# TensorE's first work on a tile of ones that VectorE fills, instead of the identity matrix

## The chip, the core and the metric

The kernel runs on one core of one Trainium2 chip. The metric is the device time of one execution in microseconds. Before the change it is 965.68 us, the median of three runs (965.58 to 966.01). Lower is better.

## The reference

Two attention layers read the same input `x` (2048 tokens of 448 numbers, 16 heads of 28), and a gate per token mixes their outputs:

```python
g = sigmoid((x * gate_w).sum(-1, keepdims=True))
return g * A(x) + (1 - g) * B(x)
```

A is linear attention with a learned feature map: each head's query and key go through a 28 x 28 matrix `w_phi`, the features are the softmax of the result beside the softmax of its negative, and the output is phi_q (phi_k^T V) over phi_q (phi_k^T 1). B is full softmax attention, with a 2048 x 2048 matrix of scores for each head and no mask. Both end in an output projection, and all of it is float32.

## The kernel before, in words

The program works through four stages.

The first projects the queries and keys of B. Each float32 operand is split into a high part, rounded to a shorter format (`XH`, `w[:, 0]`), and a low part that holds the rest (`XL`, `w[:, 1]`); a product is the sum of three matmuls, high by high, high by low and low by high. `first_units` (line 614) does this for the first 512 tokens, block by block of the 448 inputs; `proj_qk` (line 568, through the helper `run` at line 109) does it for the rest, copies the result out on ScalarE, subtracts on VectorE for the low part (`keep_qk`, lines 580 and 581), and stores both to memory (line 582). The second stage computes all of A. The third computes the values of B and the first part of the row maxima that the softmax of B needs (`mx_unit`, lines 239 to 273, on the tiles `kp` and `qp`, where line 207 subtracts two loaded tiles from one another). The fourth is a loop of 256 steps that computes scores, exponentials and weighted sums, with the remaining maxima between them.

The order of work on TensorE, VectorE, ScalarE and POOL (GpSimd) is the order in which the program writes it: line 52 names these four engines. The queue of SP (SyncE), which issues all the transfers, isn't among them. Its order is chosen by the planner of the framework when the program is built.

What matters here is the very beginning. Lines 83 and 84 allocate the tile `ident` (128 x 128, float32) and fill it with the identity matrix; `make_identity` issues two POOL instructions for it, a memset and an affine select (the profile shows them as masks.py:197 and masks.py:199). VectorE's first instruction is the memset of `red` at line 163, and POOL goes on with the memset of `part` at line 161. In `first_units`, SP issues eight loads of weights and inputs. Lines 624 and 625 then issue eight matmuls of the identity with itself into the bank of `pqs[3]`. Their result is never read: the first real matmul into that bank, at line 642, starts a new sum. That first matmul needs `w[:, 0]`, which ScalarE copies at line 628 once the weights have landed, and `XH`, which VectorE copies at line 629 once the inputs have landed; for the later blocks ScalarE does both.

The identity is used again by the transposes of lines 515, 528, 1150 and 1160.

Of the kernel before, what the change touches and what calls it, by code (L numbers as in the profile page):

```python
# [8 lines left out]
F32 = mybir.dt.float32  # L9
# [8 lines left out]
P = 128  # L18
# [18 lines left out]
def f32(ap):  # L37
    return ap.bitcast(F32)
# [3 lines left out]
def gated_mix_kernel(ctx, tc, xT, wqkB, wvB, wvA, wkAT, wqAT, phi, woA, woB,  # L42
# [7 lines left out]
    nc = tc.nc  # L50
# [4 lines left out]
    const = ctx.enter_context(tc.tile_pool(name="const", bufs=1))  # L55
# [7 lines left out]
    def ps_s(nm):  # L63
        return ps.tile([P, 512], F32, tag="s", name=nm, bufs=psn[0])

    def ps_pv(nm):
        return ps.tile([P, 512], F32, tag="pv", name=nm, bufs=1)

    def ps_mx(nm):
        return ps.tile([P, 512], F32, tag="mx", name=nm, bufs=psn[1])  # L70
# [11 lines left out]

    ident = const.tile([P, P], F32, name="ident")
    make_identity(nc, ident)
    sel_s = const.tile([P, 4], F32, name="sel_s")
    mask_s = const.tile([112, 64], F32, name="mask_s")
    z_s = const.tile([P, NT], F32, name="z_s")
# [489 lines left out]
    def keep_qk(m, t, pq, ev):  # L577
        tt = slice(t * 512, (t + 1) * 512)
        e = ev.tile([P, 2, 512], F32R, tag="ev", name=f"ev{t}_{m}")
        nc.scalar.copy(e[:, 0, :], pq)  # L580
        nc.vector.tensor_sub(e[:, 1, :], pq, f32(e[:, 0, :]))
        nc.sync.dma_start(qk_d[m * P:(m + 1) * P, :, tt], f32(e))
# [14 lines left out]
    def x_loads(t):  # L597
        loads(("x", t), lambda: load_x(t, 0), lambda: load_x(t, 2))
# [7 lines left out]
    def splits(n):  # L606

        if n % 4 == 1 and n < 12:
            split_x(n // 4 + 1, raws.pop(("x", n // 4 + 1)))
        if n in (13, 15):  # L610
            split_part(wB[1], "wB1", 384, (n - 13) // 2)
        take_lows()

    def first_units():

        raw = [stg.tile([P, 2, 512], F32, tag="stg", name=f"first_raw{b}") for b in range(3)]
        raw.append(f32(ev.tile([P, 2, 512], F32R, tag="ev", name="first_raw3")))
        for b in range(4):
            nc.sync.dma_start(raw[b][:, 0, :], wqkB[:, b, :512])
            nc.sync.dma_start(raw[b][:, 1, :], xT[:, b, :512])  # L620
        x_loads(1)
        pqs = [ps_s(f"pqk0_{m}") for m in range(3)] + [ps_pv("pqk0_3")]
        later.extend(ps_mx(f"pqk_{i}") for i in range(3))
        for _ in range(8):
            nc.tensor.matmul(pqs[3][:, :P], ident, ident, start=True, stop=True)
        for b in range(4):
            w, x = wB[0][:, :, b, :], XH[:, b, :512]
            nc.scalar.copy(w[:, 0, :], raw[b][:, 0, :])
            (nc.scalar.copy if b else nc.vector.tensor_copy)(x, raw[b][:, 1, :])
            nc.vector.tensor_sub(w[:, 1, :], raw[b][:, 0, :], f32(w[:, 0, :]))  # L630
            if b < 3:
                nc.vector.tensor_sub(XL[:, b, :512], raw[b][:, 1, :], f32(x))
                todo = [(0, x), (1, x), (0, XL[:, b, :512])]
            else:
                nc.vector.tensor_sub(x[64:], raw[b][64:, 1, :], f32(x[64:]))
                todo = [(0, x), (1, x)]
            if b < 3:
                order = [(i, m) for i in range(3) for m in range(4)]
            else:
                order = [(i, m) for m in range(4) for i in range(2)]  # L640
            for i, m in order:
                nc.tensor.matmul(pqs[m], w[:, todo[i][0], m * P:(m + 1) * P], todo[i][1],  # L642
                                 start=b == 0 and i == 0, stop=b == 3 and i == 1,
                                 skip_group_check=True)
        hold = raws[("x", 1)][0][:1, 0, :4]
        splits(1)
        nc.gpsimd.tensor_copy(phi_s[:1, :, 0], hold)
        for m in range(4):
            keep_qk(m, 0, pqs[m], ev)

    later = []
    first_units()
    pkv = ps_pv("pkv")
    for n in range(4, NP):
# [644 lines left out]
```

## Time and profile before

| | |
|---|---|
| median of three runs | 965.68 us |
| the profiled execution | 965.82 us |
| its span, first to last instruction | 964.0 us |
| TensorE busy | 959.0 us, 99% of the span |
| ScalarE busy | 741.7 us, 77% |
| VectorE busy | 712.9 us, 74% |
| POOL busy | 230.2 us, 24% |
| granted TensorE clock | 1.000 |

Times are microseconds from the span's start. PE is TensorE's matmuls and PEld its weight loads, DVE is VectorE, ACT is ScalarE, and SPq is SyncE's queue of transfers. Matmuls are pipelined and their ends are modelled, so that two records can overlap; the distance between their starts is the surer measure of pace. A row of the timeline merges neighbours of one kind: its first number is the start of the first, its second the time to the end of the last, and xN says how many there are. In brackets stands how long the engine was idle before, and what ended that.

### The profile page before, as it was taken

The numbers are of one execution on the slowest core, as the hardware profiler recorded it, in microseconds if no ns is written. First come the engines' busy times: TensorE is split into PE (matmuls) and PEld (weight loads), VectorE is DVE, ScalarE is ACT, GpSimd is POOL, SyncE is SP. The second block draws the span as 40 slices with busy tenths as digits, with TensorE's granted clock in tenths as the row PEclk, the third lists the DMA queues.
The fourth block names the chain that finished last, engine by engine and source line by source line (L and its number), as shares of the span: only waits on it lengthen the run. The fifth ranks groups of instructions, "written<-read, shape, count | busy, mean of one in ns | idle before, by whom it ended". The sixth has DMA issues, their size and how long they took to land.

```text
span 964.0 us, 22412 instructions
## 1 busy us (share of the span) xinstructions
PE 959.0 (99%) x8510; PEld 592.7 (61%) x8510; DVE 712.9 (74%) x1338; ACT 741.7 (77%) x1224; POOL 230.2 (24%) x237
## 2 busy tenths in 40 slices
PE   9999999999999999999999999999999999999998
PEld 8877877787877655555554555555555455555555
DVE  5576767789855678888888888888888888885112
ACT  4465656578866788888888898898988988887662
POOL 1235445578734800111101001001101001000010
PEclk9999999999999999999999999999999999999999
DMA  8883110023333334022132121232231222000441
GB/s 299 296 283 121 39 54 33 23 63 98 86 107 101 98 110 138 26 60 55 57 111 57 32 62 50 62 88 61 63 84 46 66 60 76 31 21 32 146 151 58
DMA packets 56620, 84.49 MB, mean 88 GB/s; under 512 B 17696, under 2 KB 24464, under 8 KB 56512
## 3 DMA queue, kind: packets, MB, share of 16 engines
q1 hardware_dynamic: 56512, 83.06, 28.4%
q8 instruction: 67, 1.10, 0.5%
q14 instruction: 41, 0.34, 0.1%
HBM read 54.86 MB, written 27.78 MB: 86 GB/s over the span
## 4 chain that ended last, share of the span: by engine, by line
PE 99%; DVE 0%; POOL 0%; issue 0%; POOLq 0%
PE pv L1061 27%; PE wide L891 18%; PE g L891 10%; PE pqk L109 6%; PE poa L109 4%; PE pk L127 4%; PE pva L127 4%; PE g L289 4%; PE pq L109 4%; PE pmd L261 4%; PE pob L109 3%; PE pvb L127 2%; PE pvb L109 2%; PE pft L528 2%; PE pqk L642 1%; PE pn L541 1%
## 5 line engine op out<-in xcount | busy, mean ns | idle before, releaser
L296 DVE TENSOR_REDUCE part<-g 128x1 f32<-128x512 f32 x704 | 442.8, 685 | 79.7 <-PE g L289 77.6
L900 ACT ACTIVATE pw<-wide 128x1024 f32<-128x1024 f32 x232 | 237.4, 1023 | 58.0 <-PE wide L891 58.0
L903 ACT ACTIVATE p<-g 128x512 f32<-128x512 f32 x510 | 277.7, 605 | 0.0
L1061 PE MATMUL pv<-p,vb 128*32 128x512 f32 x1028 | 270.0, 605 | 0.0
L1061 PE MATMUL pv<-pw,vb 128*32 128x512 f32 x1020 | 268.9, 605 | 0.0
L891 PE MATMUL g<-qst,kst 32*128 32x512 f32 x1668 | 249.9, 411 | 0.0
L891 PEld LDWEIGHTS wide<-qst,kst 32*128 32x128 f32 x1392 | 112.2, 183 | 194.5 <-ACT pw L900 190.3
L289 PE MATMUL g<-kc,qc 28*128 28x512 f32 x704 | 229.7, 489 | 0.0
L891 PE MATMUL wide<-qst,kst 32*128 32x512 f32 x1392 | 224.5, 426 | 0.0
L891 PEld LDWEIGHTS g<-qst,kst 32*128 32x128 f32 x1668 | 159.7, 183 | 21.8 <-ACT pw L903 6.7
L266 DVE CUSTOM_DVE_ANT_0 rl<-pmb,rl 128x512 f32<-128x512 f32 x160 | 103.4, 684 | 49.8 <-ACT rl L265 49.7
L412 POOL TENSOR_TENSOR oUb<-oUb,rsb 128x512 f32<-128x512 f32 x15 | 19.3, 1286 | 480.6 <-DMA rsb<-rdb 358.6
L265 ACT ACTIVATE rl<-pmd 128x512 f32<-128x512 f32 x160 | 87.3, 602 | 32.6 <-PE pmb L261 31.8
L289 PEld LDWEIGHTS g<-kc,qc 28*128 28x128 f32 x704 | 86.6, 182 | 0.1
L1061 PEld LDWEIGHTS pv<-pw,vb 128*32 128x32 f32 x1020 | 37.6, 108 | 36.2 <-issue 32.4
L109 PE MATMUL pqk<-XH,wB 128*128 128x512 f32 x192 | 59.1, 397 | 0.0
L1061 PEld LDWEIGHTS pv<-p,vb 128*32 128x32 f32 x1028 | 37.8, 108 | 29.0 <-issue 28.3
L903 ACT ACTIVATE pw<-g 128x512 f32<-128x512 f32 x46 | 26.0, 642 | 26.9 <-PE g L891 26.5
L580 ACT CAST ev<-pqk 128x512 fp32r<-128x512 f32 x28 | 16.0, 589 | 36.8 <-PE pqk L109 15.5
L109 PE MATMUL poa<-woA_s,oTa 128*128 128x448 f32 x192 | 43.4, 375 | 0.0
L1072 DVE SCALAR_TENSOR_TENSOR acc<-pob,gate,acc 128x448 f32<-128x448 f32 x12 | 8.2, 684 | 47.2 <-PE pob L109 47.2
L109 PEld LDWEIGHTS pqk<-XH,wB 128*128 128x128 f32 x192 | 35.5, 188 | 8.5 <-issue 1.5
(169 smaller groups left out, 1268.7 us busy)
## 6 DMA issues: line engine op xcount, KB each, us to landing
qkd<-ev SPq DMA_DIRECT2D x28, 512.0 KB
qst<-qkd SPq DMA_DIRECT2D x64, 112.0 KB
kst<-qkd SPq DMA_DIRECT2D x64, 112.0 KB
od<-oTb SPq DMA_DIRECT2D x48, 112.0 KB
rsa<-rda SPq DMA_DIRECT2D x32, 128.0 KB
oL<-od SPq DMA_DIRECT2D x8, 512.0 KB
rsb<-rdb SPq DMA_DIRECT2D x15, 256.0 KB
gad<-ga SPq DMA_DIRECT2D x16, 224.0 KB
```

What stands on the lines that cost most here:

```text
L109: nc.tensor.matmul(dst, l, r, start=i == 0, stop=i == len(todo) - 1)
L127: nc.tensor.matmul(dst[:, :n], l, r, start=i == 0, stop=i == len(todo) - 1, skip_group_check=True)
L261: nc.tensor.matmul(pm[j], qc[js, qt * P:(qt + 1) * P], kc[js, :], start=True, stop=True, tile_position=(32 * i, 0))
L265: nc.scalar.activation(rl, pm[i], AF.Relu)
L266: nc.vector.tensor_tensor_reduce(rl, pm[2 + i], rl, 1.0, LOWEST, ALU.add, ALU.max, part[:, col + i:col + i + 1])
L289: nc.tensor.matmul(pm, mxs[("qc", gq)][js, qt * P:(qt + 1) * P], mxs[("kc", gq // NQ, kb)][js, :], start=True, stop=True, tile_position=(3 ...
L296: nc.vector.tensor_reduce(part[:, col:col + 1], pm, AX.X, ALU.max)
L412: (nc.gpsimd if n == 1 else nc.vector).tensor_mul(oU, oU, rs)
L891: nc.tensor.matmul(st[j], kst_of[(gq // NQ, kt // 4)][js, k, (kt % 4) * P:(kt % 4 + 1) * P], qst_of[gq][js, q, :], start=n == 0, stop=n == ...
L900: nc.scalar.activation(pw, wide, AF.Exp, scale=SCALE)
L903: nc.scalar.activation(pts[s][j], st[j], AF.Exp, scale=SCALE)
L1061: nc.tensor.matmul(pv[32 * j:32 * j + 32, :], vb[kt // 8][:, kt % 8, 4 * g + j, :], pt[j], start=kt == 0, stop=kt == NT - 1, tile_position ...
```

## The change

A second constant tile, `ones`, of 128 x 128 float32, is allocated behind the identity, and VectorE fills it with 1.0. This memset becomes VectorE's first instruction, ahead of the one on `red`. The eight matmuls of line 625 read `ones` for both operands in place of `ident`. The identity is still made, for the transposes.

```diff
     ident = const.tile([P, P], F32, name="ident")
     make_identity(nc, ident)
+    ones = const.tile([P, P], F32, name="ones")
+    nc.vector.memset(ones, 1.0)
     sel_s = const.tile([P, 4], F32, name="sel_s")
...
         for _ in range(8):
-            nc.tensor.matmul(pqs[3][:, :P], ident, ident, start=True, stop=True)
+            nc.tensor.matmul(pqs[3][:, :P], ones, ones, start=True, stop=True)
         for b in range(4):
```

## The prediction

> **What bounds the kernel now.** I read four views: the page's chain of work that ended last, the waits of TensorE, the groups of its costliest instructions, and then the timeline of the first 16 us, because the change touches only what happens there.
>
> From the page:
> ```profile
> span 964.0 us, 22412 instructions
> PE 959.0 (99%) x8510; PEld 592.7 (61%) x8510; DVE 712.9 (74%) x1338; ACT 741.7 (77%) x1224; POOL 230.2 (24%) x237
> PEclk9999999999999999999999999999999999999999
> ...
> PE 99%; DVE 0%; POOL 0%; issue 0%; POOLq 0%
> ```
> From the waits, asked for TensorE alone over the whole span:
> ```profile
> PE pqk L625 <- POOL ident masks.py:199: 1.4, 1, 1.4
> ```
> The chain is TensorE for 99% of the span, and the only wait of its matmuls that the profile lists is the one in question: 1.4 us before the first matmul of line 625. Everything behind it is a queue of matmuls that hand over to one another, in step with ScalarE in the long loop. So a time won or lost at the start is carried to the end, one for one, unless a later wait on something that isn't TensorE takes it away.
>
> The start, from the timeline (start us, duration us, engine, line, operation; in brackets the idle time and what ended it):
> ```profile
> 0.74 0.20 POOL masks.py:197 MEMSET ident<- 128x128 f32 x1 [0.29 <-POOLq L1286]
> 0.84 0.17 DVE L163 MEMSET red<- 128x128 f32 x1 [0.84 <-PEq L1286]
> 1.02 0.29 POOL masks.py:199 TENSOR_SCALAR_AFFINE_SELECT ident<-ident 128x128 f32<-128x128 f32 x1
> 1.36 3.78 PE L625 MATMUL pqk<-ident 128*128 128x128 f32 x16 [1.36 <-POOL ident masks.py:199]
> 4.21 0.43 DVE L629 CAST XH<-first_raw 128x512 fp32r<-128x512 f32 x1 [3.21 <-DMA first_raw<-in_xT_dram]
> ...
> 4.51 0.63 PE L625 MATMUL pqk<-ident 128*128 128x128 f32 x2
> 4.72 0.42 PE L625 MATMUL pqk<-ident 128*128 128x128 f32 x1
> 4.76 0.30 PEld L642 LDWEIGHTS pqk<-XH,wB 128*128 128x128 f32 x1
> 4.79 0.77 PE L642 MATMUL pqk<-XH,wB 128*128 128x512 f32 x1
> 5.37 0.33 PEld L642 LDWEIGHTS pqk<-XH,wB 128*128 128x128 f32 x1
> 5.79 0.32 PEld L642 LDWEIGHTS pqk<-XH,wB 128*128 128x128 f32 x1
> 6.15 0.19 PEld L642 LDWEIGHTS pqk<-XH,wB 128*128 128x128 f32 x1
> 6.38 0.19 PEld L642 LDWEIGHTS pqk<-XH,wB 128*128 128x128 f32 x1
> ...
> 10.03 1.07 PE L642 MATMUL pqk<-XL,wB 128*128 128x512 f32 x4
> 10.94 1.98 PE L642 MATMUL pqk<-XH,wB 128*128 128x512 f32 x8
> ...
> 15.47 0.62 PE L109 MATMUL pqk<-XH,wB 128*128 128x512 f32 x2
> ```
> Three things are to be seen. First, the eight warm-up matmuls of line 625 (16 records, two each) run from 1.36 to about 4.83: the last record starts at 4.72, and from one record to the next it is 4.72 - 4.51 = 0.21 us, half of it a weight load. Second, the first real matmul (line 642) needs XH, and XH is ready when VectorE's cast ends, at 4.21 + 0.43 = 4.64; its weight load comes at 4.76, and that it waited for data and not only for the warm-up is plain from these two times. Third, the pace doubles soon after: loads at 5.37 and 5.79 are 0.42 us apart and take 0.33, those at 6.15 and 6.38 are 0.23 apart and take 0.19. The column of the granted clock says full speed all the while, so the pace has to be read from the starts. The gap from 5.79 to 6.15 (0.36) holds the switch: with x us slow in it, x/0.42 + (0.36 - x)/0.23 = 1 gives x = 0.29, so the switch is near 6.08, or 4.72 us after the first warm-up matmul.
>
> **The change part by part.**
>
> The new tile. One VectorE memset of 128x128, a twin of the one on red (0.17 us at 0.84), goes ahead of that one in VectorE's order; red moves from 0.84 to about 1.01. VectorE's next work is the cast at 4.21, after 3.21 us of idle time that a transfer ends, so the memset is free there; without that cover it would cost 0.17. The tile takes 128 x 4 = 512 bytes of each partition, and tiles allocated later in those pools lie 512 bytes further on. I cost that at nothing.
>
> The wait moved. The warm-up waited for two POOL instructions, the last ending at 1.02 + 0.29 = 1.31, and began 0.05 later. Now it waits for one VectorE instruction that ends at 0.84 + 0.17 = 1.01, so it begins near 1.06, which is 0.30 earlier. The trace has no hand-over from VectorE at this place; from below, TensorE can't start before the 1.01, and from above nothing speaks for a later start than the 1.36 of today. I take 1.06, since the kind of hand-over is that of the 0.05.
>
> Identity on TensorE later. Line 515 is then its first user:
> ```profile
> L515 PEld LDWEIGHTS pkvT<-ident,kvT x2: 138/138/139, 195.8 to 196.0; 128*128 128x128 f32 x2
> ```
> It comes at 195.8, the identity is ready at 1.31: nothing. POOL's own work stays as it is.
>
> The first real matmul. The warm-up would end near 4.53 instead of 4.83, but XH still comes at 4.64. So 0.30 us of earlier start turns into 0.23 us of idle TensorE before 4.76. What is won is only the overhang: the first load begins at 4.76 and the warm-up's tail lasts to 4.83. From below that is 0.07 us; from above it is the 0.58 us that the first matmul held TensorE (4.79 to 5.37) less the 0.42 of the next, 0.16. I take the 0.07, as the tail is the nearer row.
>
> The switch of pace. In the slow stretch a microsecond costs 1 - 0.23/0.42 = 0.45 us against the fast pace. If the switch stays at 6.08, the 0.07 us of earlier work at slow pace is worth 0.07 x 0.55 = 0.04 us. If the switch follows the first matmul at a fixed distance, it comes at 5.78, and the slow stretch behind the first matmul shrinks by 0.30: 0.30 x 0.45 = 0.14 more, 0.18 in all. One trace can't tell these two apart. What bounds any gain is the whole loss of the stretch: three matmuls took 6.15 - 4.79 = 1.36 us where 3 x 0.23 = 0.69 would do, so 0.67.
>
> A sentence apart for what the notes say: the Trainium skill, TensorE: Matmul & The Clock Gate, Part 1 (The HAM clock gate), has TensorE at half rate until an activity window of 4096 cycles at 1.2 GHz (3413 ns) was busy, and that window runs freely and doesn't start with the kernel. The trace agrees in the factor of two; by that rule a switch at 6.08 closed a window opened at 2.67, after both starts, and the sum would be the 0.04 of the first case, by the fixed distance the 0.18 of the second.
>
> Between 0.04 and 0.18 I take 0.1. It stays on the path as far as the trace shows: the later steps of this stage are ready in time (the four low-part matmuls at 10.03 and the eight at 10.94 follow each other without a gap). The profiled execution took 965.82 us for a span of 964.0, 0.14 above the median of 965.68; the sum is 965.82 - 0.1 = 965.72 for such an execution, and against the median 965.68 - 0.1 = 965.6.
>
> The transfers. Line 52 leaves only four engines in written order; the order of SP's queue is the planner's, which goes by its own idea of when things are ready. An earlier TensorE start may turn a few neighbours round in it. I cost it at nothing and keep it as a rival.
>
> **The rivals.**
>
> It changes nothing. A later wait on a transfer eats the 0.1 us. SP is nearly without a pause here and feeds the kp tiles:
> ```profile
> 44.01 0.81 SPq L176 DMA_DIRECT2D kt<-qkd  x2
> 44.92 2.10 SPq L582 DMA_DIRECT2D qkd<-ev  x3
> 46.80 1.11 DVE L207 TENSOR_TENSOR kp<-kp,kt 28x512 fp32r<-28x512 f32 x1 [0.71 <-DMA kt<-qkd]
> 48.20 0.18 PEld L261 LDWEIGHTS pmd<-kp,qp 28*128 28x128 f32 x2
> 61.87 0.19 PEld L261 LDWEIGHTS pmd<-kp,qp 28*128 28x128 f32 x2 [0.36 <-POOL kp L207]
> ```
> At 48.20 the margin behind VectorE's 46.80 + 1.11 = 47.91 is 0.29 us, and at 61.87 the weight load does wait for kp. Time: 965.7. For it: these margins; against it: SP's stores are fed by TensorE and would come earlier with it.
>
> The slow pace lasts longer. The 0.23 us of idle time between warm-up and first real matmul is new; today TensorE is busy without a break from 1.36. If the switch needs unbroken work, it counts anew from 4.76 and comes at 4.76 + 4.72 = 9.48, 3.40 us later than 6.08: 3.40 x 0.45 = 1.53 us lost, 967.2. It decides only if a pause of 0.23 in some 4.7 us breaks the count. Against it: 5% idle is little. By the rule of the notes cited above (the Trainium skill, TensorE: Matmul & The Clock Gate, Part 1) one more window would cost 3.41 x 0.45 = 1.5 us; no run here shows how full a window must be.
>
> Slower, by the order of transfers. If the planner puts the group of three ev stores (2.10 us at 44.92) ahead of the two kt loads (44.01), kp at 48.20 comes 2.10 us later against a margin of 0.29: 1.8 us. The same at 61.87, where there is no margin: 2.1 more. Together 3.9, so 969.6. It decides from an order that delays kt by over 0.29. For it: SP's order isn't written down; against it: the stores and loads here all hang on TensorE and would shift together.
>
> Faster by more than a few tenths. The switch comes at or before the first real matmul and the loss of 0.67 goes: 965.0. Beyond that only a kinder order of transfers could help, by an amount for which the matmuls' single wait gives no room.
>
> **How the numbers follow.** The forecast with a gain of 0.04 to 0.18: 0.50. Nothing gained (965.7): 0.15. Switch much earlier (965.0): 0.06. Slow pace longer (967.2): 0.10. Transfers worse (969.6): 0.12. Transfers kinder, by 2 us or more (963.7): 0.07. Left out of the range are the last two, 0.19. It therefore goes from 965.0, less 0.2 for the spread of the runs (965.58 to 966.01), to 967.2, with 0.4 above for the same spread: 964.8 to 967.6. The likeliest case's own range is 965.4 to 965.9. A measurement of this kernel tells about 0.2%, 1.93 us, from no change. Slower by more: the transfers, 0.12, and 0.02 of the longer slow pace; faster by more: 0.07; the rest, 0.79, is within.
>
> **What would show it.** In the changed kernel line 625 starts near 1.06 and waits for VectorE's memset; its last record starts near 4.42; the first load of line 642 stays at 4.7 to 4.8; the starts of line 642 turn from 0.42 to 0.23 apart between 5.7 and 6.1; line 109 first runs about 0.1 earlier than its 15.47 of today; SP's list is in the same order. Wrong would be shown by slow starts after 6.5, by a wait of line 261 on kt or kp of over 0.4 us, or by a first matmul of line 642 that moved with the warm-up.

## The result, and the profile after

The changed kernel takes 970.91 us (968.92 to 972.56), against 965.92 us for the kernel before in the same comparison: a ratio of 1.0054, with a 95% interval of 1.0043 to 1.0065. It is slower by half a per cent, where I forecast 965.6 us and no change that could be told. The profiled execution took 970.89 us for a span of 969.1.

The page of the changed kernel, first the span and the engines, then the chain:
```profile
span 969.1 us, 22413 instructions
PE 961.4 (99%) x8510; PEld 593.0 (61%) x8510; DVE 712.6 (74%) x1339; ACT 742.0 (77%) x1224; POOL 229.6 (24%) x237
...
PE 98%; DMA 1%; SPq 0%; DVE 0%; issue 0%; ACT 0%; ACTq 0%
```
One instruction more, as the diff says, and the same work on every engine. But the chain, which had no DMA in it, now has 1%. The waits of TensorE in the changed kernel (engine, tile and line, who it waited for, us in total, times, longest):
```profile
PE pqk L111 <- DVE ev L583: 2.2, 1, 2.2
PE pqk L627 <- DVE ones L86: 1.1, 1, 1.1
PE pv L1063 <- DVE oUb L390: 0.4, 1, 0.4
```
The wait at the start fell from 1.4 to 1.1 us, as meant. A new one of 2.2 us stands at line 111 (the old 109), which is the projection of the queries and keys, on a subtraction of VectorE. I look at the start first.

The timeline of the changed kernel's start (start us, duration us, engine, line, operation; in brackets the idle time and what ended it):
```profile
0.84 0.17 DVE L86 MEMSET ones<- 128x128 f32 x1 [0.84 <-PEq L1288]
...
1.06 3.78 PE L627 MATMUL pqk<-ones 128*128 128x128 f32 x16 [1.06 <-DVE ones L86]
4.07 0.43 DVE L631 CAST XH<-first_raw 128x512 fp32r<-128x512 f32 x1 [2.93 <-DMA first_raw<-in_xT_dram]
...
6.49 0.27 PEld L644 LDWEIGHTS pqk<-XH,wB 128*128 128x128 f32 x1
6.80 0.19 PEld L644 LDWEIGHTS pqk<-XH,wB 128*128 128x128 f32 x1
...
15.69 0.61 PE L111 MATMUL pqk<-XH,wB 128*128 128x512 f32 x2
```
The warm-up starts at 1.06 and XH is ready at 4.07 + 0.43 = 4.50. The pace switches in the gap from 6.49 to 6.80: by the sum of the prediction, with 0.42 and 0.23 us a matmul, at 6.67, 5.6 us after the warm-up began instead of 4.72. Line 111 first runs at 15.69, against 15.47 before: 0.2 us lost here, where I had expected 0.1 won. That is not the 5.1 us by which the spans differ (969.1 - 964.0).

The 5 us are found by walking along TensorE with one landmark after another. The first "fold" of `w_phi` into A's weights (the tile `pwk`) starts at 40.41 before and at 40.62 after; the second at 43.82 and 48.12. From one to the other it is 3.41 us before and 7.50 after: 4.09 us are lost within one stretch of work of 3.41. TensorE there, first before, then after:
```profile
40.41 1.04 PE L363 MATMUL pwk<-phi_s,wtk 112*128 112x112 f32 x8
41.22 0.70 PE L109 MATMUL pqk<-XH,wB 128*128 128x512 f32 x2
...
43.82 1.04 PE L363 MATMUL pwk<-phi_s,wtk 112*128 112x112 f32 x8
```
```profile
40.62 1.04 PE L365 MATMUL pwk<-phi_s,wtk 112*128 112x112 f32 x8
43.91 0.99 PE L111 MATMUL pqk<-XH,wB 128*128 128x512 f32 x2 [2.24 <-DVE ev L583]
...
45.12 1.05 PE L111 MATMUL pqk<-XH,wB 128*128 128x512 f32 x2
45.97 0.63 PE L111 MATMUL pqk<-XL,wB 128*128 128x512 f32 x1
46.40 1.05 PE L111 MATMUL pqk<-XH,wB 128*128 128x512 f32 x2
...
48.12 1.04 PE L365 MATMUL pwk<-phi_s,wtk 112*128 112x112 f32 x8
```
There are two losses. The matmul behind the fold comes 3.29 us after the fold's start (43.91 - 40.62) instead of 0.81 (41.22 - 40.41): a delay of 2.48. The other 4.09 - 2.48 = 1.61 us is lost after TensorE has started again: three matmuls take 46.40 - 45.12 = 1.28 us, 0.43 each, nearly twice the 0.23 of the fast pace. Here the column of the granted clock shows it too. TensorE in windows of the changed kernel (stretch, its length, PE's busy time and instructions, granted clock, share of the DMA engines, GB/s):
```profile
43.90:45.00 1.10, 1.09 (x3) 0.64 0.30 112
45.00:46.00 1.00, 1.00 (x4) 0.50 0.38 123
46.00:47.00 1.00, 1.00 (x4) 0.50 0.91 330
47.00:48.00 1.00, 1.00 (x5) 0.69 1.00 383
```
A clock of 0.64 over 1.10 us is 2 x 0.36 x 1.10 = 0.79 us at half rate; with 1.00, 1.00 and 2 x 0.31 = 0.62 of the other three rows, the half rate lasted 3.41 us. At half rate that costs 1.7 us, and 1.61 was lost.

What held TensorE is a chain of hand-overs between engines that each work in written order. ScalarE and VectorE of the changed kernel at that place:
```profile
41.43 0.83 ACT L145 CAST wB<-wB_raw 128x768 fp32r<-128x768 f32 x1 [5.01 <-DMA wB_raw<-in_wqkB_dram]
42.16 1.07 ACT L582 CAST ev<-pqk 128x512 fp32r<-128x512 f32 x2
...
42.29 0.96 DVE L146 TENSOR_TENSOR wB<-wB_raw,wB 128x768 fp32r<-128x768 f32 x1 [5.15 <-ACT wB L145]
43.17 1.28 DVE L583 TENSOR_TENSOR ev<-pqk,ev 128x512 fp32r<-128x512 f32 x2
```
ScalarE stood idle for 5.01 us on the load of half of B's last weights (`wB_raw`, 128 x 768), which nobody needs yet. Behind that copy in its order stand the copies of line 582, which empty the banks that line 111 wants to fill. They start at 42.16. VectorE is blocked in the same way: it stood idle for 5.15 us on ScalarE's copy, ahead of its own subtraction for the weights (line 146, from 42.29), and the subtractions of line 583, which the banks wait for too, stand behind that one. The first of those starts at 43.17, and TensorE starts again at 43.91. Before, the same copy of the weights ran with no wait:
```profile
36.73 0.84 ACT L143 CAST wB<-wB_raw 128x768 fp32r<-128x768 f32 x1
```
The load is late because SP's queue has another order. SP before and after (x is the number of transfers in a row):
```profile
15.10 0.39 SPq L132 DMA_DIRECT2D wB_raw<-in_wqkB_dram  x1
...
17.39 11.97 SPq L582 DMA_DIRECT2D qkd<-ev  x7
...
34.65 1.10 SPq L132 DMA_DIRECT2D wB_raw<-in_wqkB_dram  x1
```
```profile
15.87 3.55 SPq L584 DMA_DIRECT2D qkd<-ev  x4
...
21.39 6.32 SPq L584 DMA_DIRECT2D qkd<-ev  x4
...
32.79 2.37 SPq L358 DMA_DIRECT2D wtk<-in_wkAT_dram  x4
35.20 0.94 SPq L134 DMA_DIRECT2D wB_raw<-in_wqkB_dram  x2
36.24 0.88 SPq L584 DMA_DIRECT2D qkd<-ev  x1
```
Before, the first half of `wB_raw` went out at 15.10, among the first loads and ahead of all stores of `ev`. After, both halves go out at 35.20, behind ten stores and the four loads of `wtk`: 20 us later. The two kernels issue the same 673 transfers, in the same order but for places 15 to 49 of the queue (counted from 0). The other engines' orders are the same.

The chain that ended last is no help in seeing this. There the store of 36.24 (`DMA qkd<-ev`, 6.92 us) stands ahead of VectorE's subtraction, because it landed last of all that the subtraction's semaphores name. So the late store was a cause to be tested beside the late load.

### The profile page after: what moved, and what is told of

Read it like the earlier page. It is cut to its first block, busy times and chain, and to the rows that moved or that the text cites. A ratio compares the mean times of both kernels' runs of the same rounds, so it can differ in the third digit from the quotient of the medians.

```text
span 969.1 us, 22413 instructions
## 1 busy us (share of the span) xinstructions
PE 961.4 (99%) x8510; PEld 593.0 (61%) x8510; DVE 712.6 (74%) x1339; ACT 742.0 (77%) x1224; POOL 229.6 (24%) x237
## 4 chain that ended last, share of the span: by engine, by line
PE 98%; DMA 1%; SPq 0%; DVE 0%; issue 0%; ACT 0%; ACTq 0%
PE pv L1063 27%; PE wide L893 18%; PE g L893 10%; PE pqk L111 6%; PE poa L111 4%; PE pk L129 4%; PE g L291 4%; PE pva L129 4%; PE pq L111 4%; PE pmd L263 4%; PE pob L111 3%; PE pvb L129 2%; PE pvb L111 2%; PE pft L530 2%; PE pqk L644 1%; PE pn L543 1%
```

## The experiments

My theory: the new order of SP's queue, and in it the late load of `wB_raw`, holds ScalarE, hence TensorE, and the pause brings on the half clock. The rivals: the tile or its memset, the earlier warm-up, the late store, or another of the moved transfers.

**The tile alone.** The tile and its memset stay; the warm-up reads the identity again.
```diff
-            nc.tensor.matmul(pqs[3][:, :P], ones, ones, start=True, stop=True)
+            nc.tensor.matmul(pqs[3][:, :P], ident, ident, start=True, stop=True)
```


> The ones tile and its memset stay, the eight warm-up matmuls read the identity as before. SP's queue keeps the order of the kernel before. Theory 'order' (the loss comes from the new order of SP's first 50 transfers): 965.9, no wait of TensorE on line 583. Rival 'tile' (the 512 bytes or the memset cost it): 970.9.

Measured: 966.38 us, ratio 1.0002 (0.9993 to 1.0011). SP's order is that of the kernel before, and TensorE again waits 1.4 us for POOL's identity. The weight loads of its first real matmuls, where the pace switches:
```profile
7.50 0.22 PEld L644 LDWEIGHTS pqk<-XH,wB 128*128 128x128 f32 x1
7.77 0.19 PEld L644 LDWEIGHTS pqk<-XL,wB 128*128 128x128 f32 x1
```
So the tile, its 512 bytes and the memset cost nothing that can be told, and it isn't they that turn the queue round: that comes with the warm-up's new operands. The pace switched near 7.59 here, with the warm-up starting at 1.36 as in the kernel before, which switched at 6.08. The switch doesn't keep a fixed distance from the first matmul.

**The changed kernel with the old order of SP.** Edges that only fix an order, with no semaphore behind them, tie the first 52 transfers together in the order of the kernel before.
```diff
+    sent = []
+    issue = nc.sync.dma_start
+    def dma_start(*a, **k): sent.append(issue(*a, **k)); return sent[-1]
+    nc.sync.dma_start = dma_start
...
+    order = [0, 1, 2, 3, 4, 5, 6, 7, 8, 9, 14, 16, 17, 15, 18, 19, 24, 31, 48, 49,
+             10, 11, 12, 13, 20, 21, 22, 25, 23, 26, 27, 28, 29, 30, 32, 33,
+             34, 35, 36, 37, 38, 39, 40, 41, 42, 43, 44, 45, 46, 47, 50, 51]
+    info = mybir.DependencyInfo(mybir.DependencyClass.NoSync, mybir.DependencyReason.DATA)
+    for x, y in zip(order, order[1:]):
+        tc.add_manual_dep(sent[y].ins, sent[x].ins.name, info, reason="order")
```


> The changed kernel, with SP's transfers 15 to 49 put back into the order of the kernel before by edges that only order the queue. Theory 'order': 965.5 to 966.3, warm-up from 1.06, no wait behind the first fold near 40.6, no half clock after the first 8 us. Rival 'early start' (the new pause of TensorE before the first real matmul, or the data, costs it): 970.9, or at least the 0.2 us by which line 111 was later in the changed kernel (15.69 against 15.47).

Measured: 965.44 us, ratio 0.9997 (0.9988 to 1.0006), span 963.4. The whole loss is gone. Its copy of the weights and the start of its real matmuls:
```profile
35.45 0.84 ACT L153 CAST wB<-wB_raw 128x768 fp32r<-128x768 f32 x1
```
```profile
4.69 0.32 PEld L652 LDWEIGHTS pqk<-XH,wB 128*128 128x128 f32 x2
5.05 0.19 PEld L652 LDWEIGHTS pqk<-XH,wB 128*128 128x128 f32 x1
```
Everything that the change does on TensorE is in this kernel. In this execution the pace was fast nearly from the first real matmul on. What that wins, a few tenths, is less than the interval can tell from nothing.

**The kernel before with the new order.** The same edges, in the kernel before, with the order of the changed kernel.
```diff
+    order = [0, 1, 2, 3, 4, 5, 6, 7, 8, 9, 14, 16, 17, 15, 18, 10, 11, 12, 13, 19,
+             20, 21, 22, 23, 24, 29, 30, 25, 26, 27, 28, 31, 32, 33, 34, 35,
+             36, 37, 38, 39, 40, 41, 42, 43, 44, 45, 46, 47, 48, 49, 50, 51]
```


> The kernel before, warm-up on the identity, with SP's transfers 15 to 49 in the order of the changed kernel. Theory 'order': 969 to 972, with a wait of TensorE of some 2 us near 41.7 to 43.9 and, after it, a stretch at half clock of up to 3.4 us. Rivals 'tile' and 'early start': 965.9.

Measured: 971.26 us, ratio 1.0052 (1.0038 to 1.0066), the changed kernel's loss without anything else of the change. ScalarE and TensorE in its timeline:
```profile
42.24 0.83 ACT L151 CAST wB<-wB_raw 128x768 fp32r<-128x768 f32 x1 [5.49 <-DMA wB_raw<-in_wqkB_dram]
44.72 1.18 PE L117 MATMUL pqk<-XH,wB 128*128 128x512 f32 x2 [2.72 <-DVE ev L589]
```
With the run before, this settles that the queue's order is the cause: with the order goes the time, whichever tile the warm-up reads. What in the order does it is told apart by the next three.

**The new order, with one load early.** In the changed kernel, with its own order fixed, only transfer 31, the first half of `wB_raw`, is put ahead of the first four stores.
```diff
-    order = [..., 18, 10, 11, 12, 13, 19, ..., 28, 31, 32, 33, ...]
+    order = [..., 18, 31, 10, 11, 12, 13, 19, ..., 28, 32, 33, ...]
```


> The changed kernel in its new order, but with one transfer, the first half of wB1 (line 134, issued at 35.20), moved ahead of the first store of ev (15.87). Theory 'one late load' (ScalarE's copy of that half blocks the copies of ev behind it in ScalarE's queue, and so TensorE): the wait at 41.7 to 43.9 goes and the time is 965.5 to 966.5. Rival 'late store' (the profile's chain names the store of ev at 36.24): the wait stays, 970 to 971.

Measured: 965.76 us, ratio 1.0000 (0.9991 to 1.0009). Its SP queue and its copy:
```profile
14.98 0.38 SPq L55 DMA_DIRECT2D wB_raw<-in_wqkB_dram  x1
```
```profile
36.15 0.84 ACT L153 CAST wB<-wB_raw 128x768 fp32r<-128x768 f32 x1
```
One load moved, and the loss is gone. All the other transfers that the new order moves (the loads of x and phi, the stores, `wtk`, `sel`, `mask`) cost nothing that can be told, as long as this load is early.

**The new order, with the store early.** As before, but what is moved is transfer 33, the store that the chain names, ahead of `wtk` and `wB_raw`.
```diff
-    order = [..., 30, 25, 26, 27, 28, 31, 32, 33, 34, ...]
+    order = [..., 30, 33, 25, 26, 27, 28, 31, 32, 34, ...]
```


> The changed kernel in its new order, but with the store of ev that was issued at 36.24 moved ahead of the four loads of wtk (32.79), while both halves of wB1 stay late. Rival 'late store' (that store's landing holds the buffer that VectorE waits for): the wait of TensorE near 42 to 44 goes, 965.5 to 966.5. Theory 'one late load': the wait stays, 970 to 972, since ScalarE still waits for wB1, which now lands no earlier.

Measured: 974.51 us, ratio 1.0090 (1.0076 to 1.0104). Its SP queue, and the two ends of the wait:
```profile
36.94 0.94 SPq L55 DMA_DIRECT2D wB_raw<-in_wqkB_dram  x2
```
```profile
43.92 0.83 ACT L153 CAST wB<-wB_raw 128x768 fp32r<-128x768 f32 x1 [8.33 <-DMA wB_raw<-in_wqkB_dram]
46.40 1.22 PE L119 MATMUL pqk<-XH,wB 128*128 128x512 f32 x2 [5.56 <-DVE ev L591]
```
The late store falls: with it early the wait grew. Putting the store ahead pushed `wB_raw` from 35.20 to 36.94, ScalarE's copy from 41.43 to 43.92, and TensorE's restart from 43.91 to 46.40. I had sized this too small, since I hadn't counted what the early store does to the load behind it. In all three runs with the pause, TensorE starts again 2.48 us after ScalarE's copy of the weights starts (43.91 - 41.43, 44.72 - 42.24, 46.40 - 43.92): the copy is what it hangs on, by way of the steps on VectorE. (That this equals the 2.48 us of delay above is chance.)

**The old order, with the load late.** The kernel before, its order fixed, with transfer 31 moved down beside its other half.
```diff
-    order = [..., 24, 31, 48, ..., 30, 32, 33, ...]
+    order = [..., 24, 48, ..., 30, 31, 32, 33, ...]
```


> The kernel before in its own order, but with one transfer, the first half of wB1 (issued at 15.10), moved back to stand next to the second half (34.65). Theory 'one late load': ScalarE idles for some us before its copy of that half, TensorE waits 1 to 4 us near 40 to 44 and runs at half clock for 3.4 us afterwards if the pause is long: 968 to 972. If several moved transfers are needed together: 965.9.

Measured: 966.78 us, ratio 1.0009 (1.0000 to 1.0018). A miss in size, with the mechanism there. Its SP queue, ScalarE and TensorE:
```profile
32.72 2.52 SPq L55 DMA_DIRECT2D wB_raw<-in_wqkB_dram  x2
39.70 0.84 ACT L151 CAST wB<-wB_raw 128x768 fp32r<-128x768 f32 x1 [3.37 <-DMA wB_raw<-in_wqkB_dram]
42.18 0.74 PE L117 MATMUL pqk<-XH,wB 128*128 128x512 f32 x2 [0.61 <-DVE ev L589]
```
The restart is again 2.48 us behind the copy (42.18 - 39.70). But the load went out at 32.72, 2.48 earlier than in the changed kernel, so ScalarE's copy was 1.73 earlier and of TensorE's wait only 0.61 was left. The granted clock stayed at 1.00 throughout the profiled execution. The late load alone makes the wait; how long it is goes with the time at which the load is issued (32.72, 35.20 and 36.94 in these runs), and so with what the queue has ahead of it.

**Keeping TensorE at work in the pause.** The changed kernel, its order fixed, with twelve more matmuls of `ones` behind the first fold, where the pause is.
```diff
+        if n == 13:
+            awake = ps_mx("awake")
+            for _ in range(12):
+                nc.tensor.matmul(awake[:, :P], ones, ones, start=True, stop=True)
```


> The changed kernel in its new order, with twelve more matmuls of the ones (128x128, into a bank of their own) behind the first fold, where TensorE waits; their result is not used. At full pace they take about 12 x 0.21 = 2.6 us, about the length of the wait. If the loss is the wait (2.2) and, beside it, the half clock that the pause brings (3.4 us, worth 0.45 each, 1.5 us): the wait stays, no half clock follows, and the time is 1 to 1.9 us below the changed kernel, 969.0 to 969.9. If the half clock costs nothing of its own: 970.9 or above.

Measured: 969.15 us, ratio 1.0034 (1.0021 to 1.0046), 1.76 below the changed kernel (0.0020 by the two ratios, 1.9 us). Its ScalarE and TensorE, and then the window from 44 to 46 us:
```profile
40.78 0.83 ACT L153 CAST wB<-wB_raw 128x768 fp32r<-128x768 f32 x1 [5.20 <-DMA wB_raw<-in_wqkB_dram]
40.66 2.86 PE L694 MATMUL awake<-ones 128*128 128x128 f32 x24
43.28 0.71 PE L119 MATMUL pqk<-XH,wB 128*128 128x512 f32 x2
```
```profile
44.00:46.00 2.00, 2.00 (x11) 1.00 0.62 176
```
The load is as late, the copy as late to its place, and yet no half clock. From fold to fold it took 6.10 us (39.78 to 45.88), 2.69 over the 3.41 of before: the delay alone. So the loss has two terms, shown apart: some 2.5 us of pause and some 1.6 of half clock brought on by it.

**A mend in the source.** The changed kernel, with the line that loads the weights moved up by two steps of the program, and the planner free.
```diff
+            part_loads("wB1", wqkB[:, :, 512:896], 384, "wB1")
...
-        if n == 10:
-            part_loads("wB1", wqkB[:, :, 512:896], 384, "wB1")
```


> The changed kernel, with the loads of wB1 written at unit 8 instead of unit 10 and no edges: the planner then queues them ahead of phi and wtk, behind the eighth store of ev. Theory 'one late load': ScalarE's copy of the first half no longer waits, no wait of TensorE near 42 to 44, 965.3 to 966.2, the same as the kernel before. If the stores and the other loads of the new order matter too: above 967.

Measured: 967.09 us, ratio 1.0013 (1.0004 to 1.0022). The new wait of its TensorE:
```profile
PE pqk L111 <- POOL XH L334: 0.6, 1, 0.6
```
Some 3.8 us come back (970.91 - 967.09). The copy of the weights runs at 35.46, waits for nothing, and there is no half clock between 40 and 54 us. A miss of about 1 us against what I expected: TensorE waits 0.6 us for what POOL makes of the last quarter of x, and 0.4 us for `oUb` much later. POOL in this run:
```profile
34.78 0.18 POOL L356 COPY wtk<-phi_s 1x4 f32<-1x4 f32 x1 [14.66 <-DMA phi_s<-in_phi_dram]
...
36.30 1.26 POOL L334 TENSOR_TENSOR XH<-xraw,XH 64x512 fp32r<-64x512 f32 x1
```
It is the same trap on another engine. The load of `phi` now goes out behind both halves of `wB_raw`, at 28.47, and POOL stands idle for 14.66 us on it. The subtraction that TensorE waits for stands behind that copy in POOL's order and ends at 36.30 + 1.26 = 37.56; the matmul starts at 37.61. The x that it reads had been there for long: ScalarE's copies of it start between 25.5 and 27.0. None of the versions beats the kernel before by more than can be told.

## Why the prediction was wrong, point by point

**The start was right where it was priced by rows.** The memset runs at 0.84 and costs nothing; the warm-up starts at 1.06, as put; XH still sets the first real matmul; the identity's later readers cost nothing; the 512 bytes cost nothing (the tile alone, 1.0002). With the old queue the changed kernel takes 965.44 us, near the forecast 965.6. Whether the 0.1 us is won or nothing changes, that interval (0.9988 to 1.0006) can't tell.

**The switch of pace was wrong in both of my cases.** It came neither at 6.08 nor at 5.78, but at 6.67. The trace also keeps a record of the clock, and its first entry agrees: it stands at 6.65 here, at 6.05 in the kernel before and at 7.57 with the tile alone. In the ten traces the first entry comes 2.8 to 6.2 us after the warm-up's start. A fixed distance falls. This agrees with the rule cited in the prediction (the Trainium skill, TensorE: Matmul & The Clock Gate, Part 1), by which the window runs freely. It makes the start worth some tenths of a microsecond more or less from one trace to the next. The rival "the slow pace lasts longer", with its switch at 9.48, falls too: of the six traces with the `ones` warm-up none has it later than 6.65. The break of 0.23 us itself wasn't seen ahead of a switch, though: in three of these traces the switch came before the break, and in the other three the weight loads broke off for 0.07 to 0.14 us only.

**The step that failed** is "The transfers": "An earlier TensorE start may turn a few neighbours round in it. I cost it at nothing and keep it as a rival." The queue changed not in a few neighbours but in places 15 to 49, and one load moved down by 20 us. I gave that rival 0.12 and a time of 969.6; the time came out at 970.91, but by another mechanism. I looked for the price among the `kt` loads at 44.01 and the `kp` waits of 48.20 and 61.87; in the changed kernel these matmuls have no wait on `kp` or `kt` at all. It was a load that TensorE didn't need yet, whose copy and subtraction stand in ScalarE's and VectorE's order ahead of those that empty the banks. That TensorE would wait for nothing later held for the order of before alone.

What would have shown it beforehand: SP's timeline from 13 to 36 us, with the first half of `wB_raw` out at 15.10 and the second at 34.65, together with ScalarE's copy at 36.73. A load that goes out some 20 us early, in a queue with hardly a pause, with its reader in the middle of an in-order engine: that margin is large only as long as the planner leaves it there. In the kernel before, the second half's copy, at 42.73, already waited 0.69 us for its load. With the order of SP not written down, any edit that touches the planner's idea of readiness can move it.

**The sum, as measured.** Of the 5.1 us of span, 0.2 come from the start (the pace switched later in this execution), 2.5 from TensorE's pause, 1.6 from the half clock behind it, and the rest, 0.8, lies near the end: the 0.4 us wait on `oUb` in the table of waits, and as much behind the last group of matmuls (964.25 to the end at 969.1, against 959.56 to 964.0). What makes either I haven't settled. The wait appears in three of the other runs too, among them one without the pause at line 111, and it wasn't taken apart.

Why the planner turns the queue round is only argued: the tile alone leaves it, so it goes with the warm-up reading `ones`, and in the planner's idea the warm-up no longer waits for POOL's identity. I haven't seen the reckoning behind its choice.

## What to carry to other kernels

Where one queue's order is left to a planner, compare that queue transfer by transfer after every edit, however far from it the edit is: here an edit on TensorE and VectorE that costs nothing by itself moved one load by 20 us, and the time by 0.54%. Look at each load's reader: one that stands in an in-order engine ahead of work that TensorE waits for needs a wide margin, or its place written down. Here that was ScalarE and VectorE, and POOL when the load was written earlier. And don't take the last name in the chain of waits for the cause without moving it alone; here that name was a store, and moving it made things worse.

## What the runs showed of the hardware

A short pause can cost most of its own length again. After 2.24 us without matmuls the granted clock fell to 0.50 for 3.41 us, and 1.61 us went with that; after a pause of 0.61 us it stayed at 1.00. The length of 3.41 us agrees with the window that the Trainium skill gives (TensorE: Matmul & The Clock Gate, Part 1, 3413 ns). The rule in the same page's section HAM oscillation — how this bites in real kernels, that TensorE's gaps should not be longer than about 3.4 us, doesn't hold here: 2.24 us was enough.

The clock doesn't fall when the pause has reached some length, but at ticks that the pause doesn't set. By the sum over the four windows it fell at 45.00 - 0.79 = 44.21, which is 2.5 us after the last matmul ended (40.62 + 1.04 = 41.66) and 0.3 us after TensorE had started again. In the kernel before with the new order it fell 2.8 us after the last matmul (42.00 to 44.79), with the store early 4.1 us after (40.84 to 44.94, and there for 6.83 us). In these three traces each fall, and each return, comes a whole number of 3.413 us after the first entry of the clock's record (6.65, 7.25 and 3.98). So it matters where a pause lies between two ticks. With the store early, 0.69 us of the pause lay ahead of the tick at 44.94 - 3.41 = 41.53, and the clock stayed; how much it takes, between 0.69 and 2.24 us, no run here shows.

Nor does every execution lose the half clock. Of the six of the changed kernel, one took 968.92 us at a mean clock of 1.000, three 970.40 to 970.94 at 0.998, and two 972.5 at 0.995 and 0.996. With TensorE kept at work in the pause, five executions took 968.59 to 969.67, at 0.999 or 1.000. So without the half clock the new order costs some 3 us of the median's 5, and the rest comes with the half clock; that the ticks decide between the six is likely, but only the one of 970.89 has a trace.

The slow pace at the start of the kernel (0.42 us a matmul) isn't seen in the column of the granted clock, which says full speed there; at 45 us the column shows it. The column is made from the trace's record of the clock, which has no entry ahead of the first switch (6.65 in the changed kernel). So the pace at the start has to be read from the distance of the starts, or from that first entry.
